# Folding the sign of the imaginary filter into its copy, and loading the third sequence of a Fourier filter and snake MLP kernel at other steps

## Chip, cores and metric

One core of one Trainium2 chip. The metric is the device time of one launch in microseconds, median of the runs shown. The kernel takes float32 inputs, works in float16 between the matmuls, and writes float32.

## The reference

```python
def _attn_ref(x, filt_r, filt_i):            # x: (8, 3008, 256), filters: (1505, 256)
    X = np.fft.rfft(x, axis=1)
    F = (filt_r + 1j * filt_i)[None, :, :]
    Y = X * F
    y = np.fft.irfft(Y, n=x.shape[1], axis=1)
    return y.astype(np.float32)

def _moe_ref(x, w_in, w_out, alpha):         # x: (24064, 256), w_in: (256, 2048)
    h = x @ w_in
    s = np.sin(alpha * h)
    g = h + s * s / (alpha + 1e-09)
    return (g @ w_out).astype(np.float32)
```

The second function takes the first one's result, 8 sequences of 3008 rows with 256 channels each, as one block of 24064 rows.

## The kernel before

**The spectral part** filters one sequence ("batch" b, 0 to 7) at a time. The length 3008 is split as 94 x 32, and the transform is done in four matmul stages with transfers between them.

- `load_x(b, ch)` (L138) loads a quarter of x on the POOL queue, and casts it to float16 on the way. From batch 2 on, the load waits for the last instruction of the MLP part that DVE was given before it (`marks["snake"]`, the STT below).
- `first(i)`, i = 0 to 15 (L178): one matmul `pa`, an eviction to `t1_h`, and after every fourth a store to the DRAM tile d1, on the SP queue (L186).
- `load_t2(g)`, g = 0 to 3 (L189): two POOL loads from d1, which turn rows into partitions.
- `forward(u)`, u = 0 to 11 (L196): two matmuls `pb`, an ACT cast to `xf`, and two SP transfers that write the halves of `xf` into `xs` with real and imaginary partitions crossed.
- `product(u)` and `cross(u)` (L211, L219): the complex product on DVE. `xf` times `f_t[0]`, plus `xs` times `f_t[1]`. `cross` waits for the transfers into `xs`.
- `inverse(w)` (L224): two matmuls `pc`, an eviction to `g`, and after every third two SP stores to the DRAM tile d2 (L239).
- `load_t4(ch)` (L242): a load from d2 on SP into the tile that the profile calls `t_a`.
- `last(u)`, u = 0 to 15 (L247): four matmuls `pd` and an eviction into columns of `y`, the input of the MLP part.

Batch 0 goes another way in a head of some 37 us: it turns tiles with DVE transposes, and multiplies by both filters in one instruction (L441), with the two products added by two accumulating matmuls, against the tables `e_t` and `e1_0`. `last_0` (L321) makes its columns of `y`, most of them spread one by one between the matmuls of the first steps; its half `cb` = 0 is evicted on ACT, `cb` = 1 on DVE.

The filter tile `f_t[k]`, k = 0 real and k = 1 imaginary, is loaded into half of the partitions only. `other_half(g, k, on_act)` (L383) copies it to the other half on DVE, in two groups g of 12 rows. Before the change the copy of the imaginary part is plain. The product of batch 0 wants it plain, with the sign in the table `e1_0`: `inverse_table` (L363) multiplies by a column `sign` of 0.125 and -0.125 (L360 to L362). The later batches want the lower half negated; `negate(i)` (L600) does that in place, after the products of batch 0, in two DVE instructions of 64x3072 (L603).

**Evictions.** `evac` (L157) puts PSUM into SBUF on ACT or DVE. Without an order from the caller, every third call goes to DVE and the others to ACT. Each call moves this count on, also one whose engine is ordered.

```python
        flip[0] = (flip[0] + 1) % 3
        if flip[0] if on_act is None else on_act:
```

**The MLP part** goes through y in 48 chunks of 512 columns (four of them of 384). `hidden(k, jb)` (L534) makes one of 16 blocks of a chunk: two accumulating matmuls `ph`, a cosine on ACT (L545), and one SCALAR_TENSOR_TENSOR on DVE (L546, "STT" below) into `v`. `project(k, u)` (L550) multiplies v by the second weights, 8 matmuls `po` each; after 16 or 32 of them ACT copies the result out (L566) and `store` sends it off (L586). For the first five chunks all these stores are issued on POOL, later ones on SP. The PSUM pools are `hps` with 4 slots for ph, `fps` with 2 slots for all spectral stages after the head, and `ops` with 2 slots for po.

**The order** is written out by hand. Time is counted in steps, 8 to a chunk. A step gives out two `hidden` blocks of chunk k and up to one `project` of chunk k - 1 (8 po). Everything else is a list of pairs "due step, piece" (`put`, L594). `slot(step)` (L634) runs between the two and `slot(step + 0.5)` at the end of the step; each gives out all pieces due, but stops at a second piece with matmuls unless that one is late by a step or more. Because the list is sorted by due step, a piece behind such a stop waits too. Every engine and every DMA queue works through its own pieces in the order in which they were given out. A step takes about 1.7 to 2.2 us.

In this order the pieces around the change fall as follows before it. The negates are given out at the end of step 13 and in the middle of step 14, around the evictions of `last_0`. The matmuls pa of batch 1 fall in steps 7 to 13, those of batch 2 in steps 36 to 47: the last one right after the ph of step 47. The loads of x of batch 2 fall in steps 22, 27, 32 and 37. The two crossed copies `xs` of batch 1 go out from step 17 (u = 0) to 31 (u = 11); its stores to d2 in steps 26, 30, 33 and 37, its loads of t4 in steps 38 (three) and 45. On SP the first d1 store of batch 2 stands just ahead of these three. The loads of t2 of batch 2 are given out in step 47, on POOL just ahead of the output store of chunk 4 (its second half: eight DMAs). The first pd of batch 1 is at the end of step 43, the first pb of batch 2 at the end of step 53.

Of the kernel before, what the change touches and what calls it, by code (L numbers as in the profile page):

```python
# [10 lines left out]
FP32 = mybir.dt.float32  # L11
# [3 lines left out]
ALU = mybir.AluOpType  # L15
# [47 lines left out]
def kernel(  # L63
# [10 lines left out]
    nc = tc.nc  # L74
# [17 lines left out]
    def pool(name, bufs, space=None):  # L92
        kw = {} if space is None else {"space": space}
        return ctx.enter_context(tc.tile_pool(name=name, bufs=bufs, **kw))

    cpool = pool("consts", 1)
# [18 lines left out]
    def by_half(t):  # L115

        return t.rearrange("p a (b c) -> p (a b) c", c=128)
# [16 lines left out]
    f_t = [filt_t[:, k] for k in range(2)]  # L134
# [22 lines left out]
    def evac(dst, src, on_act=None):  # L157
        flip[0] = (flip[0] + 1) % 3
        if flip[0] if on_act is None else on_act:
            marks["act"] = nc.scalar.copy(out=dst, in_=src)  # L160
        else:
            marks["dve"] = nc.vector.tensor_copy(out=dst, in_=src)  # L162
# [108 lines left out]
    e1_0 = by_half(t4_h[1])  # L271
# [24 lines left out]
    for g in range(2):  # L296
        gs = slice(12 * g, 12 * g + 12)
        for k, filt in enumerate((filt_r, filt_i)):
            for q in range(2):
                if (g, k, q) == (0, 1, 1):  # L300
# [3 lines left out]
                    out=f_t[k][64 * k + 32 * q:64 * k + 32 * q + 32, gs, :],  # L304
# [52 lines left out]
        nc.tensor.transpose(out=ps[:, 0:16], in_=rec, identity=id32)  # L357
        nc.vector.tensor_scalar(out=rec_t, in0=ps[:, 0:16], scalar1=-0.5, scalar2=None, op0=ALU.mult)

    sign = cpool.tile([128, 1], FP32)  # L360
    nc.vector.memset(sign[0:64], 0.125)
    nc.vector.memset(sign[64:128], -0.125)  # L362

    def inverse_table(g):

        gs = slice(8 * g, 8 * g + 8)
        ps = ops.tile([128, 8, 128], FP16, name=f"pse_{g}", tag="o")
        for i in range(8):
            for a in range(2):
                nc.tensor.transpose(out=ps[64 * a:64 * a + 64, i, :],  # L370
                                    in_=d_t[:, 8 * g + i, 64 - 64 * a:128 - 64 * a], identity=id16)
        nc.scalar.mul(e1_0[:, gs, :], ps, sign)

    warmed = []

# [7 lines left out]
    def other_half(g, k, on_act):  # L383

        gs = slice(12 * g, 12 * g + 12)
        evac(f_t[k][64 - 64 * k:128 - 64 * k, gs, :], f_t[k][64 * k:64 * k + 64, gs, :], on_act)

    warm_pe(10)
    def cast_x0(h):
# [6 lines left out]
    for i in range(16):  # L396
        own, tag = (fps, "f") if i % 3 == 2 else (hps, "h")
        ps = own.tile([128, 512], FP32, name=f"pa_0_{i}", tag=tag)
# [21 lines left out]
    for i in range(4):  # L420
        turn(t2_0[i // 2][:, :, 32 * (i % 2):32 * (i % 2) + 32], t1_0[:, :, 32 * i:32 * i + 32])
        if i > 1:
            other_half(0, i - 2, False)
# [56 lines left out]
    def weights_in(g):  # L480
# [4 lines left out]
        if g == 0:  # L485
            after(ins, marks["products"])

    [inverse_table(g) for g in range(2)]
    for i in range(6):
        forward_0(i)  # L490
        if i % 3 == 2:
            if i == 2: inverse_table(2)
            warm_pe((4, 0)[i // 3])
    for i in range(13):
        for e in {5: [(1,0,False)],6: [(1,1,False)]}.get(i, ()):
            other_half(*e)
        if i < 12:
            product_0(i)
        if i == 11:
            reciprocals()  # L500
        if i > 0:
            inverse_0(i - 1)
        if i + 6 < 12:
            forward_0(i + 6)
        if i == 12:
            turn_back(0)
# [87 lines left out]
    def put(at, fn, *args, pe=False):  # L594
        pending.append((at, len(pending), pe, fn, args))
# [1 line left out]
    for jb in range(12, 16):  # L597
        put(5 + 0.5 * (jb - 12), weights_out, jb, 1)

    def negate(i):  # L600

        gs = slice(12 * i, 12 * i + 12)
        nc.vector.tensor_scalar(out=f_t[1][0:64, gs, :], in0=f_t[1][0:64, gs, :],  # L603
                                scalar1=-1.0, scalar2=None, op0=ALU.mult)

    for i in range(2):
        put(13 + i, negate, i)
    for n0, n, at in ((6, 5, 1.5), (11, 4, 12.5), (15, 4, 14), (19, 4, 15.5), (23, 4, 17), (27, 5, 19)):
        put(at, last_0, n0, n, fps, "f", True)
    for b in range(1, B):  # L610
        s = s1 if b == 1 else Spectral(b)
        z = 48 * b
        if b > 1:
            for ch in range(4):
                put((22,27,32,37)[ch] if b == 2 else z - 92 + 7 * ch, s.load_x, ch)
        for i in range(16):
            put(6.9 + 0.35 * i if b == 1 else 36 + 0.66 * i if b == 2 else z - 67 + 0.66 * i, s.first, i, pe=True)
        for g in range(4):
            put(12.5 if b == 1 else max(z - 56, 46.5), s.load_t2, g)
        for u in range(12):  # L620
            inv = 23.5 + 1.25 * u if b == 1 else 59 + 2.1 * u if b == 2 else z - 40.8 + 2.3 * u
            fwd = inv - (6 if b == 1 else 6)
            put(fwd, s.forward, u, pe=True)
            put(fwd + (0.5 if b == 1 else 1.5), s.product, u)
            if s.fused:
                put(fwd + (4 if b == 1 else 4.5), s.cross, u)
            put(inv, s.inverse, u, pe=True)
        for ch in range(4):
            put(z - (9.5 if b == 1 and ch < 3 else (10.5, 10.5, 10.5, 3)[ch]), s.load_t4, ch)
        for u in range(16):  # L630
            put(z + (u - (5 if b == 1 else 6.5) if u < 4 else 2 * u - 9), s.last, u, pe=True)
# [59 lines left out]
```

## Time and profile before

| what | value |
|---|---|
| median of 3 runs | 785.87 us (785.68 to 786.81) |
| profiled execution | 785.97 us, its span 784.2 us |
| instructions | 16646 |
| granted TensorE clock, mean | 0.999 |
| ph matmuls (L541) | 1536, 387.8 us busy |
| po matmuls (L558) | 3008, 389.5 us busy |
| STT on DVE (L546) | 768, mean 671 ns |
| negate on DVE (L603) | 2, mean 946 ns |
| filter copies on DVE (L162, 64x3072) | 4, mean 956 ns |
| table multiplies on ACT (L372) | 3, mean 1126 ns |
| loads of x (L141) | 32, median 5.0 us from issue to landing |

The busy times of matmuls overlap, since they are pipelined; the time from one start to the next is what counts. In the timeline and in the chain of waits a row has a start and a length in microseconds, an engine (SPq and POOLq are the instructions that issue DMAs), a line of the kernel and a count. A `sign` or `filt_t` in a row is the tile's name in the program; `d` is d1 or d2, told apart by the line; `t` is t2 and `t_a` holds t4. In the windows, a row begins with the stretch and its length, then comes the busy time of PE, PEld, DVE, ACT and POOL with the number of instructions, the granted clock, the share of the DMA engines and GB/s.

### The profile page before, as it was taken

What the parts mean: (1) busy time and instruction counts of PE and PEld (TensorE: products, weight loads), DVE (VectorE), ACT (ScalarE), POOL (GpSimd) and SP (SyncE); (2) the same over time, 40 slices, a digit from 0 to 9 for tenths busy, and PEclk for the clock granted to TensorE, in tenths of its full rate; (3) what the DMA queues carried; (4) which work ended last, traced back from release to release, by engine and by line L of the source; (5) the groups of instructions that cost most, each with busy time, mean ns of one, the idle gap of its engine ahead of it and who ended that gap; (6) DMA issues with size and microseconds to landing.
All of it is one profiled execution on the core that took longest, in us unless ns stands there. A gap on an engine that the chain in (4) does not pass through costs nothing.

```text
span 784.2 us, 16646 instructions
## 1 busy us (share of the span) xinstructions
PE 771.1 (98%) x5799; PEld 535.2 (68%) x5799; DVE 655.7 (84%) x1169; ACT 617.6 (79%) x1211; POOL 113.3 (14%) x190
## 2 busy tenths in 40 slices
PE   7999999999999999999999999999999999999998
PEld 4757766676667766777666766767667776766666
DVE  7897996899878997799877998799977999777773
ACT  5797987888878887888877887788887887777674
POOL 6456443500020000200020000200002000000000
PEclk9999999999999999999999999999999999999999
DMA  9956577755564546654575454835556243421112
GB/s 214 281 112 164 124 142 213 158 124 121 163 174 89 129 105 190 148 122 108 131 202 114 103 115 131 226 87 118 119 161 176 65 98 80 117 61 29 41 41 54
DMA packets 86655, 100.99 MB, mean 129 GB/s; under 512 B 14896, under 2 KB 74294, under 8 KB 86572
## 3 DMA queue, kind: packets, MB, share of 16 engines
q1 hardware_dynamic: 74644, 71.11, 33.4%
q0 software_dynamic: 11712, 28.78, 19.4%
q8 instruction: 45, 0.74, 0.4%
q14 instruction: 38, 0.31, 0.1%
q10 hardware_dynamic: 216, 0.05, 0.0%
HBM read 55.72 MB, written 46.66 MB: 131 GB/s over the span
## 4 chain that ended last, share of the span: by engine, by line
PE 92%; DVE 3%; DMA 1%; ACT 1%; issue 1%; SPq 0%; ACTq 0%; DVEq 0%
PE po L558 40%; PE ph L541 39%; PE pa L181 3%; PE pd L254 2%; PE pb L201 2%; PE pc L232 2%; DVE v L546 2%; PE pc L453 1%; DMA al<-in_moe_alpha_dram 1%; ACT cos_all L545 1%; PE warm L381 1%; PE pb L431 1%; DMA t_a<-d 0%; SPq L586 0%; PE pa L399 0%
## 5 line engine op out<-in xcount | busy, mean ns | idle before, releaser
L546 DVE SCALAR_TENSOR_TENSOR v<-cos_all,ph 128x512 f16<-128x512 f32 (+1 forms) x768 | 482.9, 671 | 106.8 <-ACT cos_all L545 103.6
L545 ACT ACTIVATE cos_all<-ph 128x512 f32<-128x512 f32 (+1 forms) x768 | 411.2, 592 | 95.3 <-PE ph L541 94.3
L558 PE MATMUL po<-w,v 128*128 128x256 f16 x3008 | 389.5, 272 | 0.0
L541 PE MATMUL ph<-y,w 128*128 128x512 f16 (+1 forms) x1536 | 387.8, 374 | 1.6 <-DVE y L162 0.9
L558 PEld LDWEIGHTS <-v 128*128 128x128 f16 x3008 | 288.3, 98 | 78.3 <-issue 2.0
L541 PEld LDWEIGHTS <-w 128*128 128x128 f16 x1536 | 147.9, 98 | 103.9 <-issue 3.1
L566 ACT COPY o<-po 128x512 f32<-128x512 f32 (+1 forms) x97 | 55.6, 573 | 19.9 <-PE po L558 13.5
L586 POOL DMA_DIRECT2D out_dram<-o x67 | 35.0, 529 | 207.6 <-ACT o L566 205.4
L193 POOL DMA_DIRECT2D t<-d x56 | 36.3, 664 | 180.4 <-DMA out_dram<-o 98.7
L204 ACT CAST xf<-pb 128x512 f16<-128x512 f32 x84 | 50.0, 595 | 13.1 <-PE pb L201 12.3
L141 POOL DMA_DIRECT2D x<-in_x_dram x32 | 17.1, 537 | 259.7 <-PE pc L232 146.5
L160 ACT CAST t_h<-pa 96x512 f16<-96x512 f32 x74 | 43.3, 585 | 8.8 <-PE pa L181 8.5
L160 ACT CAST y<-pd 128x376 f16<-128x376 f32 (+1 forms) x82 | 39.5, 482 | 8.8 <-PE pd L254 5.3
L254 PEld LDWEIGHTS <-t_a 96*128 96x128 f16 x448 | 31.3, 97 | 19.8 <-DMA t_a<-d 1.4
L181 PE MATMUL pa<-x,wf_t 94*96 94x512 f16 x112 | 42.4, 381 | 0.6 <-ACT t_h L160 0.4
L160 ACT CAST g<-pc 128x512 f16<-128x512 f32 x61 | 36.2, 593 | 8.2 <-PE pc L232 7.8
L254 PE MATMUL pd<-wi_t,t_a 96*128 96x94 f16 x448 | 37.1, 204 | 1.1 <-DMA t_a<-d 1.1
L222 DVE TENSOR_TENSOR p<-p,xs 128x512 f16<-128x512 f16 x84 | 35.7, 425 | 2.9
L221 DVE TENSOR_TENSOR xs<-xs,filt_t 128x512 f16<-128x512 f16 x84 | 35.0, 417 | 0.0
L215 DVE TENSOR_TENSOR p<-xf,filt_t 128x512 f16<-128x512 f16 x84 | 35.0, 417 | 0.0
L201 PE MATMUL pb<-t,d_t 128*128 128x256 f16 x168 | 32.1, 272 | 0.2
L232 PE MATMUL pc<-p,e_t 128*128 128x256 f16 x168 | 32.1, 272 | 0.0
(66 smaller groups left out, 285.8 us busy)
## 6 DMA issues: line engine op xcount, KB each, us to landing
x<-in_x_dram POOLq DMA_DIRECT2D x30, 376.0 KB, 5.0
d<-t_h SPq DMA_DIRECT2D x28, 384.0 KB
t<-d POOLq DMA_DIRECT2D x56, 192.0 KB, 4.7
xs<-xf SPq DMA_DIRECT2D x168, 64.0 KB
d<-g SPq DMA_DIRECT2D x56, 192.0 KB
t_a<-d SPq DMA_DIRECT2D x28, 384.0 KB
out_dram<-o SPq DMA_DIRECT2D x92, 80.0 KB
w_out<-in_moe_w_out_dram SPq DMA_DIRECT2D x2, 1024.0 KB
```

Source lines behind the costliest of these rows:

```text
L160: marks["act"] = nc.scalar.copy(out=dst, in_=src)
L181: marks["pe"] = nc.tensor.matmul(out=ps[0:NK, :], lhsT=wf_t, rhs=self.x[ch][:, 2 * j:2 * j + 2, :], start=True, stop=True)
L193: nc.gpsimd.dma_start(out=self.t2[g][64 * p:64 * p + 64, :, :], in_=self.d1[a0:a0 + 6, :, :].rearrange("s n c -> n s c"))
L201: nc.tensor.matmul(out=ps[:, i, :], lhsT=d_t[:, s, :], rhs=self.t2[s // 6][:, s % 6, :], start=True, stop=True)
L204: nc.scalar.copy(out=self.xf[u], in_=ps)
L232: nc.tensor.matmul(out=ps[:, i, :], lhsT=e_t[:, 2 * w + i, :], rhs=pt[:, i, :], start=(k == 0), stop=(k == len(pr) - 1))
L254: nc.tensor.matmul(out=psv[:, i, :], rhs=wi_t, start=True, stop=True, lhsT=t4_h[ch // 2][0:NK, n0 % 16 + i, cb * 128:cb * 128 + 128])
L541: nc.tensor.matmul(out=ps[:, 0:n], lhsT=w1[:, cb, jb * 128:jb * 128 + 128], rhs=y_cols[:, cb, c0:c0 + n], start=(cb == 0), stop=(cb == 1))
L545: nc.scalar.activation(out=cs[:, 0:n], in_=ps[:, 0:n], func=AFT.Sin, bias=float(np.pi / 2))
L546: marks["snake"] = nc.vector.scalar_tensor_tensor(out=v[k][:, jb, 0:n], in0=cs[:, 0:n], scalar=-1.0, in1=ps[:, 0:n], op0=ALU.add, op1=ALU. ...
L558: nc.tensor.matmul(out=pso[k][:, t % 2, :], lhsT=v[k][:, jb, 128 * t:128 * t + 128], rhs=w2[:, jb, :], start=(jb == 0), stop=(jb == 15))
L566: nc.scalar.copy(out=o[:, i0:t % 2 + 1, :], in_=pso[k][:, i0:t % 2 + 1, :])
```

## The change

The imaginary filter's copy to the lower partitions is made with the factor -1 in the head, on DVE. The two `negate` instructions after batch 0 and their places in the order are gone. The table `e1_0` of batch 0 takes the factor -0.125 on all partitions, and the `sign` column with its two memsets is gone. `other_half` for k = 1 no longer calls `evac`, so two calls fewer move its count.

The loads of x of batch 2 get the due steps 22, 26, 30 and 34, its first stage 37 + 0.63 i in place of 36 + 0.66 i, and its loads of t2 step 47 in place of 46.5. For the later batches `z - 56` is the same number as before.

```diff
-    sign = cpool.tile([128, 1], FP32)
-    nc.vector.memset(sign[0:64], 0.125)
-    nc.vector.memset(sign[64:128], -0.125)
-
     def inverse_table(g):
...
-        nc.scalar.mul(e1_0[:, gs, :], ps, sign)
+        nc.scalar.mul(e1_0[:, gs, :], ps, -0.125)
...
     def other_half(g, k, on_act):
 
         gs = slice(12 * g, 12 * g + 12)
-        evac(f_t[k][64 - 64 * k:128 - 64 * k, gs, :], f_t[k][64 * k:64 * k + 64, gs, :], on_act)
+        if k == 0:
+            evac(f_t[0][64:128, gs, :], f_t[0][0:64, gs, :], on_act)
+        else:
+            nc.vector.tensor_scalar(out=f_t[1][0:64, gs, :], in0=f_t[1][64:128, gs, :],
+                                    scalar1=-1.0, scalar2=None, op0=ALU.mult)
...
-    def negate(i):
-
-        gs = slice(12 * i, 12 * i + 12)
-        nc.vector.tensor_scalar(out=f_t[1][0:64, gs, :], in0=f_t[1][0:64, gs, :],
-                                scalar1=-1.0, scalar2=None, op0=ALU.mult)
-
-    for i in range(2):
-        put(13 + i, negate, i)
...
-                put((22,27,32,37)[ch] if b == 2 else z - 92 + 7 * ch, s.load_x, ch)
+                put(22 + 4 * ch if b == 2 else z - 92 + 7 * ch, s.load_x, ch)
         for i in range(16):
-            put(6.9 + 0.35 * i if b == 1 else 36 + 0.66 * i if b == 2 else z - 67 + 0.66 * i, s.first, i, pe=True)
+            put(6.9 + 0.35 * i if b == 1 else 37 + 0.63 * i if b == 2 else z - 67 + 0.66 * i, s.first, i, pe=True)
         for g in range(4):
-            put(12.5 if b == 1 else max(z - 56, 46.5), s.load_t2, g)
+            put(12.5 if b == 1 else 47 if b == 2 else z - 56, s.load_t2, g)
```

## The prediction

> **What bounds the kernel now.** I read the page's shares first.
>
> ```profile
> PE 771.1 (98%) x5799; PEld 535.2 (68%) x5799; DVE 655.7 (84%) x1169; ACT 617.6 (79%) x1211; POOL 113.3 (14%) x190
> ...
> PE 92%; DVE 3%; DMA 1%; ACT 1%; issue 1%; SPq 0%; ACTq 0%; DVEq 0%
> ```
>
> TensorE is busy for 98% of the span and is 92% of the chain of waits, so an instruction taken off DVE is worth only what PE waits for it. I therefore cut the trace into steps (at the first ph matmul of each) and set each against its own work at full pace: 4 ph take 0.86 to 0.87 us at 512 columns and 0.65 at 384, 8 po 0.88, a pa 0.22, a pd 0.04. From step 9 to the end nearly every step is within 0.05 us of that. The large exceptions that the change can touch are steps 15, 16 and 43. Steps 14, 15, 16, 42 and 43, by windows (length, then each engine's busy time and instructions):
>
> ```profile
> 61.16:63.23 2.07, 2.07 (x21) 1.84 (x20) 1.92 (x3) 1.88 (x5) 0.00 (x0) 1.00 0.45 125
> 63.23:65.81 2.58, 2.24 (x24) 1.91 (x23) 2.40 (x4) 1.68 (x4) 0.28 (x1) 1.00 0.29 95
> 65.81:68.93 3.12, 2.22 (x23) 1.90 (x22) 1.94 (x4) 1.98 (x4) 3.12 (x6) 1.00 0.61 165
> 120.40:122.15 1.75, 1.75 (x15) 1.29 (x14) 1.49 (x4) 1.22 (x3) 0.00 (x0) 1.00 0.71 264
> 122.15:125.36 3.21, 2.08 (x20) 1.38 (x18) 1.34 (x3) 2.04 (x5) 0.40 (x1) 1.00 0.93 244
> ```
>
> Steps 14, 15 and 16 hold the same matmuls (4 ph, 8 pd, 8 po: 2.07 us); 15 and 16 lose 0.51 and 1.05. Step 43 holds 0.65 + 0.22 + 0.88 + 0.16 = 1.91 and takes 3.21: it loses 1.30. The clock column is 1.00, so none of it is clock. The chain of waits names both causes, first the two steps:
>
> ```profile
> 63.41 0.69 DVE v L546
> 64.09 0.86 DVE filt_t L603
> 64.96 0.46 DVE y L162
> 65.42 1.19 DVE v L546 x2
> 66.61 0.47 DVE y L162
> 67.08 0.04 issue
> 67.12 0.38 PE ph L541
> ```
>
> L603 is the second negate. It pushes back the y cast, two STTs and the next y cast, for which the ph at 67.12 waits: that ph reads these columns of y. In step 43 the chain runs over a load of t4, and the SP and POOL timelines show why it is late:
>
> ```profile
> 121.22 0.12 PE pa L181
> 121.33 3.80 DMA t_a<-d
> 125.13 0.05 issue
> 125.18 0.34 PE pd L254 x4
> ```
>
> ```profile
> 113.15 1.57 SPq L239 DMA_DIRECT2D d<-g  x2
> 115.62 0.32 SPq L186 DMA_DIRECT2D d<-t_h  x1
> 121.33 1.48 SPq L244 DMA_DIRECT2D t_a<-d  x3
> ```
>
> ```profile
> 113.60 0.52 POOL L141 DMA_DIRECT2D x<-in_x_dram  x1 [0.88 <-PE pa L181]
> ```
>
> The last store of d2 is issued in two halves at 113.15 and 114.15; the loads of t4 behind it wait for both. By the landing records the first half is in at 116.39, the second only at 121.19. Between them lies x chunk 3, issued at 113.60: its packets fill the engines from about 115.2 to 118.8, and the second half sends none from 115.9 to 118.8. In the same way the store issued at 105.11 sent nothing until 108.4, behind x chunk 2 (issued 104.89). A transfer that arrives behind an x chunk waits some 3 us here.
>
> **Negate gone: -0.47 us.** Two DVE instructions of 0.946 go from 61.45 and 64.01. The first costs nothing: the STT after it starts at 62.47, when its cosine is done at 62.44. Without the second, the y cast runs 64.01 to 64.55, the next STT at 64.55 (cosine done 64.51), but the one after it waits for its own cosine, which ACT finishes at 65.44 behind another y cast. It ends at 66.15, the needed y cast at 66.60, and ph starts near 66.65 instead of 67.12. So of 1.89 us of DVE work and 1.56 us of stall 0.47 comes back; then ACT is last. Bounds: 0.2, if the next limit bites (batch 1's first t2 pair lands at 70.36, and its pb starts at 70.83, so 0.47 ahead is the end of that cover; the d1 store before it goes out 0.2 later, see below), and 0.9, if the slot wait of 0.34 in step 15 goes as well. A PE wait of 0.33 just behind that pb, for an ACT cast, hides a late pb of that size, so I keep 0.47.
>
> **The sign in the head: 0.** The copies of filt_i cost 0.956 each (64x3072 COPY), a multiply of that shape is the negate's own row, 0.946: two times -0.01. The two memsets of 0.06 end at 3.26, ahead of 1.95 us in which DVE waits for x. The three ACT multiplies (1.126 each) read a constant in place of a column; no row shows that form, but the plain ACT copy of 512 (0.587) is within 0.03 of half of 1.126, and none of the three is in the chain: 0, bounds -0.1 and +0.1.
>
> **The rotation moves: 0.** Two calls of evac fewer in the head shift the three-beat rotation between ACT and DVE: each automatic eviction on DVE passes to the one before it in order. In steps 7 to 13 DVE then takes the casts i = 0, 3, 6, 9, 12, 15 of batch 1 instead of 1, 4, 7, 10, 13. For i = 15 the cast ends at 62.14 instead of 61.94, so the store of d1 and the loads of t2 behind it go 0.2 later (the bound above). For i = 0 it stands behind two STTs until 49.30; if the third pa took that PSUM slot it would start at 49.35 instead of 48.37, a stall of 0.98. But where an ACT slot came free first, PE in this trace waits for ACT (the pa at 52.72 does, though the older slot was DVE's), so I take 0. Later steps that lose 0.12 to 0.25 (at 195.1, 286.0, 290.4, 453.0, 564.1, 568.5) depend on the same rotation and go to other batches; six of them are 1.2 us, so half a microsecond either way is the bound.
>
> **x of batch 2 earlier: -1.30 us.** Each load is issued once its step's last STT is done plus 0.5. Chunk 3 goes from 113.60 to about 107.7, with packets from 109 to 112.3, clear of the d2 store at 113.15. That store then lands near 117 (the first d2 store's 768 packets took 2.1 us, 92.29 to 94.40). The loads of t4 also pass the d1 store of chunk 0, which moves behind them on SP; it was issued long before 121.33 and held them up by nothing, and now waits itself until about 118.5, with no reader before step 48. First t4 landing: 117.1 + 3.80 = 120.9. It is due at 123.85 (125.18 less 1.30), so 3 us to spare and the whole 1.30 returns. Lower bound 0: the store lands as late for another reason.
>
> The price is that chunks 1 and 2 now go at about 91.8 and 99.9, into the d2 stores issued at 90.96 and 99.19 and the crossed copies xs behind them, for which DVE waits in order with all STTs queued behind. xs 7 has its data at 95.05 and is read at 99.37, xs 10 at 103.90 and 107.20. One x chunk in front (3.2 us) leaves 1.1 and 0.1: hidden, just. Without that cover each further microsecond is a DVE stall.
>
> "DMA: Bandwidth & Descriptors" of the Trainium skill, section "Queues, rings and completion order", says that each engine takes turns between its queue rows packet by packet. By that rule the POOL load could not shut out SP's store; the empty stretch of 2.9 us in the trace differs, and the measurement decides. By the rule alone a separation of the two would save less.
>
> **First stage later: +0.2 us.** Sixteen pa move by a step on a PE that does them anyway. But the last pa of batch 2 goes from the start of step 47 to its end, and is cast by DVE: its d1 store goes out near 134.2 instead of 133.21 and lands near 137.2 (136.19 before). The loads of t2 move from step 47 to 48, and on POOL that is past the output store of chunk 4: eight issues of 0.52 to 0.55, 4.2 us, ready at 134.1 + 0.3. So t2 starts near 138.57 instead of 136.87. Its first pair landed at 141.16 and would at 142.86; pb of step 53 is due at 142.65. Stall 0.2; bounds 0 and 1.0 (if these stores take the 4.95 us from 142.02 to 146.97 that they took behind t2).
>
> **Sum.** -0.47 - 1.30 + 0.20 = -1.57. The profiled execution took 785.97 us (span 784.2 and 1.77 around it), 0.10 above the median of 785.87. From the median: 784.3.
>
> **Rivals.** *The t4 stall stays:* what speaks for it is that only one store in the trace shows the block from so near; against, the same hold behind chunk 2. Then -0.47 + 0.2: 785.6. *A lost slot or late t2:* the pa of step 8 waits for DVE, +0.98 (against: the pa at 52.72), or t2 lands a microsecond late: 785.2. *Slower, by crossing copies:* chunks 1 and 2 hit stores and xs together. The worst hold in the trace is the second half above, 4.4 us late against a landing near 116.8; with 1.4 us more of d2 packets in front xs 7 and xs 10 are 5.8 late and overrun their cover by 1.5 and 2.5. Less some 0.7 each that four ph slots cover, that is 2.6: 786.9. It decides from about 5 us of delay; against it, xs 8 behind chunk 1 today lands only 1.2 later than its neighbours.
>
> **Numbers.** Forecast 0.60 (own range 783.6 to 784.9), t4 stays 0.14, slot or t2 0.15, slower 0.11. The bound of 0.2% is 1.57 us, about what a measurement of this kernel can tell from no change, so the forecast sits on it. Faster: about three quarters of the forecast, 0.47, as the bounds of the negate and the rotation reach further below than above. Same: the rest and the two middle rivals, 0.43. Slower by over 0.2%, at least 787.44: 0.10. The range reaches down to the forecast with the rotation's half microsecond and 0.4 more from the negate (783.4), and up to 786.2.
>
> **What will show it.** Step 43 near 1.9 us with no wait on t_a, and the last d2 store's second half landing near 117. Step 16 near 2.6 with y's cast ending 0.5 earlier, behind a cosine. POOL's eight stores ahead of t2 near 134, and a pb wait of a few tenths in step 53. DVE without waits at the reads of xs 7 and xs 10. Wrong, if PE waits for xs, if step 8 grows by a microsecond, or if the loads of t4 are still issued near 121.

## The result, and the profile after

The changed kernel takes 784.76 us in the median of 12 runs (783.84 to 786.17). In the same comparison the kernel before takes 786.43 us (785.68 to 788.10, 12 runs): a ratio of 0.9977, 95% interval 0.9968 to 0.9986. A second comparison, made with the last experiments, gave 785.37 against 786.75 us, 0.9982 (0.9974 to 0.9991). So about 0.2% of the time is gone, just at the size that this kernel's measurement can tell. The profiled execution took 784.61 us, its span 782.8 us where it was 784.2.

The shares first, on the page of the changed kernel:

```profile
PE 771.7 (99%) x5799; PEld 535.3 (68%) x5799; DVE 654.4 (84%) x1165; ACT 617.0 (79%) x1211; POOL 113.3 (14%) x190
...
PE 93%; DVE 2%; POOL 1%; ACT 1%; DMA 1%; issue 1%; SPq 0%; ACTq 0%; POOLq 0%; DVEq 0%
```

PE's busy time is what it was; a percent of the chain passed from DVE to PE, and POOL has one now, which it had not before. The same five steps as before the change (14, 15, 16, 42, 43), by windows: the stretch and its length, then the busy time of PE, PEld, DVE, ACT and POOL, the granted clock, the DMA share and GB/s.

```profile
61.45:63.52 2.07, 2.07 (x21) 1.83 (x20) 1.71 (x3) 1.46 (x4) 0.00 (x0) 1.00 0.28 87
63.52:65.72 2.20, 2.20 (x24) 1.91 (x22) 1.82 (x3) 1.67 (x4) 0.00 (x0) 1.00 0.49 145
65.72:68.78 3.06, 2.23 (x24) 1.91 (x23) 1.84 (x3) 2.00 (x5) 2.87 (x5) 1.00 0.43 129
120.20:121.95 1.75, 1.75 (x15) 1.28 (x13) 1.47 (x4) 0.87 (x2) 0.00 (x0) 1.00 0.71 202
121.95:123.86 1.91, 1.91 (x18) 1.46 (x17) 1.03 (x3) 1.71 (x4) 0.00 (x0) 1.00 1.02 380
```

Steps 15 and 16 together went from 5.70 to 5.26, and step 43 from 3.21 to 1.91, its full pace. The chain of waits of the changed kernel in steps 15 and 16 (start, length, engine, line):

```profile
64.20 0.61 ACT cos_all L545
64.81 0.43 ACT y L160
65.23 0.51 ACT cos_all L545
65.74 0.02 issue
65.77 0.69 DVE v L546
66.46 0.47 DVE y L162
66.92 0.04 issue
66.97 0.38 PE ph L541
```

Where the second negate stood, two cosines with a y cast between them are now in the chain: ACT came to be last, as forecast, so of the DVE time taken out only these tenths return. For step 43, the SP timeline of the changed kernel, and the POOL timeline with its x chunks (start, length of the row, line, count, idle time before):

```profile
112.78 1.57 SPq L239 DMA_DIRECT2D d<-g  x2
116.64 1.87 SPq L244 DMA_DIRECT2D t_a<-d  x3
118.62 2.85 SPq L186 DMA_DIRECT2D d<-t_h  x2
```

```profile
107.69 0.52 POOL L141 DMA_DIRECT2D x<-in_x_dram  x1 [2.55 <-DVE v L546]
...
132.87 4.16 POOL L586 DMA_DIRECT2D out_dram<-o  x8 [4.96 <-ACT o L566]
137.10 5.20 POOL L193 DMA_DIRECT2D t<-d  x8
```

x chunk 3 goes at 107.69, clear of the store of d2 at 112.78, whose second half lands at 116.48 by the landing records (121.19 before); t4 is issued at 116.64 and lands at 120.33, 3.4 us ahead of its pd at 123.69. The last two rows are the output stores that t2 now stands behind.

A thing that was not forecast is at step 9. The chain there, and two rows of the waits around it:

```profile
48.06 1.85 POOL w L514
49.92 0.02 issue
49.94 1.28 DVE v L546 x2
51.23 0.61 DVE t_h L162
51.84 0.04 issue
51.88 0.38 PE pa L181
```

```profile
DVE v L546 <- POOL w L514: 1.0, 1, 1.0
...
PE pa L181 <- DVE t_h L162: 0.4, 1, 0.4
```

An STT waits 1.0 us for POOL's last multiply of the second weights (L514), because its `v` takes the buffer that held them; the cast of a pa stands behind it on DVE, and a pa waits for that cast. Worked out for each step as its length less its matmuls at full pace, what PE lost in the two profiled executions:

| steps | before, us | after, us | difference | forecast |
|---|---|---|---|---|
| up to the first ph (its time) | 36.86 | 36.52 | -0.34 | 0 |
| 9 | 0.04 | 0.60 | +0.56 | 0 (rotation) |
| 15 and 16 | 1.66 | 1.21 | -0.45 | -0.47 |
| 41 and 60 | 0.31 | 0.25 | -0.06 | 0 (rotation) |
| 43 | 1.35 | 0.05 | -1.30 | -1.30 |
| 53 | 0.05 | 0.05 | 0 | +0.20 |
| 80, 126, 128, 212, 270, 272 | 1.20 | 0.24 | -0.96 | 0 (rotation) |
| 68, 84, 116, 174, 176, 260 | 0.23 | 1.24 | +1.01 | 0 (rotation) |
| all steps | 21.91 | 20.82 | -1.09 | -1.57 |

"All steps" begins with the first ph; what it holds beyond the rows above is +0.11, spread over small ones. The full pace is taken a little tighter than the common spacing, so that a step without a stall still shows 0.03 to 0.05; by the median spacing of each kind of matmul the two sums are 9.3 and 8.2, and the differences in the table are the same to 0.05. Only differences are used below. The rows of step 60 and later are the rotation of evictions: small stalls that change places. The first row differs from launch to launch: over the 14 profiled executions of this study the first ph starts between 36.26 and 39.40 us, in no order of the kernels. So two rows answer to the forecast to a few hundredths, and two were wrong in opposite directions.

### The profile page after: what moved, and what is told of

Read it like the earlier page. It is cut to its first block, busy times and chain, and to the rows that moved or that the text cites. A ratio compares the mean times of both kernels' runs of the same rounds, so it can differ in the third digit from the quotient of the medians.

```text
span 782.8 us, 16640 instructions
## 1 busy us (share of the span) xinstructions
PE 771.7 (99%) x5799; PEld 535.3 (68%) x5799; DVE 654.4 (84%) x1165; ACT 617.0 (79%) x1211; POOL 113.3 (14%) x190
## 4 chain that ended last, share of the span: by engine, by line
PE 93%; DVE 2%; POOL 1%; ACT 1%; DMA 1%; issue 1%; SPq 0%; ACTq 0%; POOLq 0%; DVEq 0%
PE po L558 41%; PE ph L541 40%; PE pa L181 3%; PE pd L254 2%; PE pb L201 2%; PE pc L232 2%; POOL w L514 1%; PE pc L453 1%; DMA al<-in_moe_alpha_dram 1%; DVE v L546 1%; PE warm L377 1%; PE pb L431 1%; SPq L586 0%; POOL w L482 0%; PE pa L399 0%
```

## Experiments

Each was run beside the kernel before on the same chip, and compared with it. "Stalls" below are PE's losses by step as in the table, from the profiled execution; they tell a few tenths of a microsecond apart, which medians with intervals of 0.1% do not. In most comparisons the medians lie further apart than the stalls (1.56 against 0.43 us for the times of batch 2 alone, 2.52 against 1.74 for the best order below). The one trace of the kernel before is of an execution of 785.97 us, and its medians beside the experiments are 786.4 to 786.8; what those executions lose more, no trace here shows.

**The sign alone.** The changed kernel with the times of batch 2 as before, and with one line that puts the rotation back:

```diff
             nc.vector.tensor_scalar(out=f_t[1][0:64, gs, :], in0=f_t[1][64:128, gs, :],
                                     scalar1=-1.0, scalar2=None, op0=ALU.mult)
+            flip[0] = (flip[0] + 1) % 3
...
-                put(22 + 4 * ch if b == 2 else z - 92 + 7 * ch, s.load_x, ch)
+                put((22,27,32,37)[ch] if b == 2 else z - 92 + 7 * ch, s.load_x, ch)
```

> The sign alone, with the eviction rotation and batch 2's steps as before. Theory (the second negate held up the y cast and ACT is next): steps 15 and 16 together lose 1.15 to 1.25 us against 1.56 to 1.66 before, ph of step 16 still waits for the y cast, behind a cosine of ACT; step 43 keeps its stall of 1.3; time 0.3 to 0.6 us lower, a ratio of 0.9993 to 0.9996, too small to tell by time alone. Rival (all DVE time comes back): both stalls vanish, 1.6 us, ratio 0.998. Step 9: if its stall of 0.56 in the changed kernel comes from the rotation, it is absent here; if it comes from w_out's load landing late on this launch, it is here whenever POOL's last weight multiply ends later than about 49.3 us.

786.33 against 786.76 us, ratio 0.9992 (0.9980 to 1.0004). Steps 15 and 16 lose 1.22, 0.44 less than before; step 43 keeps a stall (1.57), and step 9 has none, which tells little, as POOL's last multiply ended only 11.23 after the first ph in this launch (13.39 in the changed kernel's). The negate is worth what its chain says, and the 1.89 us of DVE work are not.

**The times of batch 2 alone.** The kernel before with the changed due steps of x, first stage and t2, and with its negates.

> Batch 2's steps alone, negates kept. Theory (x chunk 3 no longer stands before the last d2 store): step 43 at 1.9 us, t4's first load issued 4 us earlier against its step, no wait for xs 7 and xs 10, pb of step 53 without a wait or with less than 0.3; steps 15 and 16 lose 1.6 as before; time 1.0 to 1.4 us lower, ratio 0.9982 to 0.9987. Rival (crossing copies or late t2 take it back): a DVE wait before the reads of xs of 1 us or more, or a pb wait of 0.5 or more in step 53, ratio above 0.9995.

785.20 against 786.76 us, 0.9975 (0.9965 to 0.9986). Step 43 is at 0.05, and steps 15 and 16 as before. But step 53 loses 0.94, which it does not in the changed kernel: its first pair of t2 lands at 141.49, where the one of the changed kernel lands at 141.04.

**x chunk 3 alone, and the first stage alone.** In the one the kernel before has its x loads at (22, 27, 32, 34), in the other its first stage and t2 go a step later and x stays at (22, 27, 32, 37).

> Only x chunk 3 of batch 2 moves, from step 37 to 34; chunk 2 stays at 32. Theory: this alone frees the last d2 store, which lands within 3.5 us of its first issue instead of 8; step 43 at 1.9 us, time 1.1 to 1.4 us lower, ratio 0.9982 to 0.9987. Rival (the order of the t4 loads and the d1 store on SP, moved by the later first stage, is what counts): step 43 keeps 1 us or more of stall, ratio above 0.9993.

785.91 us, 0.9980 (0.9965 to 0.9994). Step 43 loses 0.05, step 53 too: chunk 3 by itself frees the stall.

> Only the first stage and the t2 loads of batch 2 move; the x chunks stay at 22, 27, 32, 37. Theory: the last d2 store still waits behind x chunk 3, step 43 keeps a stall of 1.0 to 1.4 us; t2 starts behind the store on POOL as in the changed kernel, pb of step 53 waits 0 to 0.3; ratio 0.9997 to 1.0005. Rival (SP order counts): step 43's stall gone, ratio near 0.9985.

785.51 us, 0.9978 (0.9967 to 0.9989). Here the theory fell: step 43 has no stall either. The POOL and SP timelines of this run show why:

```profile
112.86 0.52 POOL L141 DMA_DIRECT2D x<-in_x_dram  x1 [0.31 <-PE ph L541]
```

```profile
112.76 1.58 SPq L239 DMA_DIRECT2D d<-g  x2
119.20 1.28 SPq L244 DMA_DIRECT2D t_a<-d  x3
```

Chunk 3 is issued at 112.86, 0.74 earlier than before the change, since fewer pieces stand ahead of it in the list. It now goes 0.10 behind the first half of the d2 store, where before the change it is 0.45 (113.60 and 113.15). The store's packets go out beside those of x, sparsely at first, and both halves wait (landed at 118.49 and 119.05); but the second is in 6.3 us after the first issue and not 8.0, and t4 is in at 122.98, half a microsecond ahead of its pd at 123.50. The stall of 1.30 hung on some 0.35 us in the place of a load against a store. Step 53 loses 0.74 here.

**Is it the d1 store that holds t4?** The kernel before, with its first three loads of t4 ahead of the d1 store of batch 2's chunk 0 on SP:

```diff
-            put(z - (9.5 if b == 1 and ch < 3 else (10.5, 10.5, 10.5, 3)[ch]), s.load_t4, ch)
+            put(z - (10.1 if b == 1 and ch < 3 else (10.5, 10.5, 10.5, 3)[ch]), s.load_t4, ch)
```

> The kernel before with one pair of SP's queue swapped: the three t4 loads of batch 1 ahead of batch 2's first d1 store. x chunk 3 stays at step 37. Theory (two transfers delay the last d2 store: x chunk 3 keeps its second half out, and then that half shares the engines with the d1 store's packets): the second half lands 1.5 to 2.5 us earlier than 8.0 us after the first issue, t4's first load lands 2 us earlier, and step 43 keeps 0 to 0.3 us of its 1.35: ratio 0.998 to 0.9988. Rival (the forecast's reading, x chunk 3 alone, the d1 store holds up nothing): 1.2 to 1.4 us stay, ratio 0.9995 to 1.0005.

785.81 against 786.62 us, 0.9986 (0.9975 to 0.9996). The SP timeline and the chain of this run:

```profile
113.20 1.57 SPq L239 DMA_DIRECT2D d<-g  x2
121.33 1.25 SPq L244 DMA_DIRECT2D t_a<-d  x3
122.69 0.35 SPq L186 DMA_DIRECT2D d<-t_h  x1
```

```profile
121.27 0.06 PE pa L181
121.33 3.61 DMA t_a<-d
124.94 0.05 issue
124.98 0.34 PE pd L254 x4
```

The loads stand first and are still issued at 121.33, for the second half of the d2 store lands at 121.17 as before (x chunk 3 is issued at 113.66). Step 43 loses 1.10 in place of 1.35: a load of 3.61 in place of 3.80 is all that comes back. What holds the store is the x chunk.

**The rotation alone.** The kernel before, with a line that moves the count as the change does:

```diff
+        flip[0] = (flip[0] - k) % 3
```

> The kernel before with the eviction count set as in the changed one, and nothing else. Theory (the cast i = 3 of batch 1 on DVE stands behind STTs that wait for POOL's last w_out multiply): steps 8 and 9 lose 0.67 in all if that multiply ends less than 12.3 us after the first ph, and 0.5 to 0.6 more if it ends 13.4 us after it; of the late small stalls six of 0.1 to 0.25 move to other steps, their sum within 0.3; step 43 keeps 1.35 and steps 15 and 16 lose 1.6 or 0.2 more; ratio 0.9997 to 1.0007. Rival (the rotation costs a PSUM slot at step 8 in every launch): step 8 or 9 1.0 us longer wherever that multiply ends.

786.05 against 786.62 us, 0.9992 (0.9979 to 1.0004). Steps 8 and 9 lose what they lose before; the slot rival of the forecast, 0.98 in step 8, is not there. The late small stalls are in just the places of the changed kernel. And a group is new: steps 40, 41, 42, 44, 47 and 48 lose 1.33 together, where they lose 0.31 before. Step 16 loses 0.14 more than before. Step 43 is at 0.05, for two reasons: PE comes to it later by the new stalls, and chunk 3 goes out 0.16 behind the d2 store's first half (113.91 and 113.75), so that the second half is in 6.45 us after the first issue. t4 lands at 124.40, by 1.1 us sooner than before when both are counted from the first ph, and is there for the pd at 125.00:

```profile
113.91 0.52 POOL L141 DMA_DIRECT2D x<-in_x_dram  x1 [0.58 <-PE ph L542]
```

```profile
113.75 1.58 SPq L239 DMA_DIRECT2D d<-g  x2
120.35 1.77 SPq L244 DMA_DIRECT2D t_a<-d  x3
```

The chain at step 40:

```profile
116.43 1.29 DVE v L547 x2
117.72 0.61 DVE t_h L162
118.32 0.04 issue
118.36 0.38 PE pa L181
```

It is the picture of step 9: the rotation puts a cast of the first stage on DVE behind two STTs, and a pa waits for it. The changed kernel has only 0.22 of this (step 41).

**POOL's order in the head.** The changed kernel, with the first load of batch 1's x one multiply later, so that POOL gets on while that load waits for the second weights to land:

```diff
-    for step in ([(weights_in, g) for g in range(3)] + [(s1.load_x, 0), (weights_in, 3), (s1.load_x, 1),
-                 (weights_in, 4), (s1.load_x, 2), (weights_in, 5), (s1.load_x, 3)]
+    for step in ([(weights_in, g) for g in range(4)] + [(s1.load_x, 0), (weights_in, 4), (s1.load_x, 1),
+                 (weights_in, 5), (s1.load_x, 2), (s1.load_x, 3)]
```

> The changed kernel with two of POOL's pieces reordered in the head: the fourth and the later weight multiplies go ahead of the x load that waits for w_out's landing. Theory (POOL sat idle for that landing, and its last multiply ends too late for the STTs of step 8): the last w_out multiply ends 1 to 2 us earlier against the first ph, at 10.5 to 12 us after it; step 9 at its 2.13 us without stall in this launch; the x loads of batch 1 are not waited for; ratio to before 0.9970 to 0.9978. Rival (step 9's stall is the rotation's alone): step 9 keeps 0.5 us or more.

784.44 against 786.62 us, 0.9972 (0.9962 to 0.9981). The stall of step 9 is gone (0.04), though in this launch the load of x came free later than in the changed kernel's (38.09, that is 1.52 after the first ph, against 0.66). Step 36 has a new 0.18: DVE waits 0.51 us there for the crossed copy xs 10, and the pc behind it waits for DVE.

**More of steps 15 and 16.** The changed kernel, with the `last_0` pieces of steps 12.5 and 14 due at 11.5 and 13, and batch 1's inverse stage slightly later.

> The changed kernel with two groups of batch 0's last stage a step earlier, and batch 1's forward and inverse stage a half step later. Theory (the ph of step 16 waits for the y cast of a group that is made in step 15, with ACT last in the chain): with that group made in step 14, steps 15 and 16 lose under 0.3 us together in place of 1.2; the pb of batch 1 waits for nothing; ratio to before 0.9962 to 0.9972. Rival (two PSUM slots are too few for pa and pd in one step, or t2 lands too late for pb): step 13 or the step of the first pb gains 0.7 us or more, ratio above 0.9975.

786.29 us, 0.9994 (0.9985 to 1.0004): the gain of the change is gone. Steps 15 and 16 lose 0.08 together, as hoped; but step 13 loses 1.96, step 20 0.65 (0.27 in the changed kernel) and step 32 0.24. The waits of PE around step 13:

```profile
PE pa L181 <- DVE t_h L162: 0.8, 1, 0.8
PE pd L343 <- ACT t_h L160: 0.5, 1, 0.5
```

The pa of batch 1 and the pd of batch 0 share the two slots of `fps`, and one step earlier they meet there.

**The last four** belong together. First the changed kernel again:

> The changed kernel once more, whole, to see which of its stalls are the order's and which the launch's. Theory: step 43 free (near 0.05), step 16 near 1.04 and step 15 near 0.17 in every launch, but the 0.56 of step 9 varies with the landing of w_out (0.56 if POOL's last multiply of w_out ends 13.2 us or more after the first ph, nothing if it ends before 12.5), and step 53 varies between nothing and 0.9 with the landing of the last d1 store and t2. Ratio 0.997 to 0.998. Rival: the 0.56 of step 9 belongs to the order and comes back at the same size whenever POOL's multiply ends.

The ratio is given above. Step 43 loses 0.05, steps 15 and 16 1.21, step 9 0.45, step 53 0.17 (0.05 in the first profile; the first pair of t2 landed 4.18 us after the first issue, where it was 3.94). The 0.45 fits the size of POOL's lateness, not a fixed price: counted from the first ph, POOL's last multiply ended at 13.24 here, at 13.39 in the changed kernel's first profile (0.60) and at 13.23 in the run with the earlier `last_0` pieces (0.45). Less 0.04, each is what the end lies beyond 12.83. With 12.38, 11.82 and 11.20 (three other kernels with the moved rotation) step 9 loses 0.04. Without the moved rotation an end at 13.76 (the first stage alone) costs nothing, and one at 14.15 (chunk 3 alone) costs 0.30: the bound there is about 1.0 us later.

Then POOL's order as above with the sign, and the two things left over crossed: the rotation put back or moved, and the first stage with t2 of batch 2 as before (x at 22, 27, 32, 34) or a step later (x at 22, 26, 30, 34).

> The parts that paid alone: sign in the copy with the rotation put back, x of batch 2 at 22, 27, 32 and 34 with its first stage and t2 as before, and the w_out multiplies on POOL ahead of the last x loads of batch 1. Theory: -0.44 (steps 15, 16), -1.30 (step 43), steps 9, 41 and 53 without a new stall, so 1.7 to 1.8 us below the kernel before on the same chip, ratio near 0.9977, a few tenths below the changed kernel. Rival: the last stores and loads of POOL decide anew, and one of steps 9, 36 or 53 takes 0.5 us or more; then no better than the changed kernel.

> As e10_parts with one line less: the rotation of evictions moves as in the changed kernel. Theory: with POOL's multiplies early the rotation's price in step 9 is gone, and only small stalls change places (41 appears, 60 goes, the late ones move to 68, 84, 116, 174, 176 and 260): within 0.3 us of e10_parts, either sign. Rival: the rotation costs half a microsecond whatever POOL does.

> All of the changed kernel but its rotation, which is put back, and with POOL's w_out multiplies early: against e10_parts it is the first stage and t2 of batch 2 a step later (and x at 22, 26, 30, 34) alone. Theory: the price of the later t2 belongs to the order and shows wherever PE comes to step 53 without having lost time before it: a stall of 0.5 to 0.9 in step 53, as in e2_times and e4_first (0.94, 0.74), so 0.5 to 0.9 above e10_parts, 784.7 to 785.2. Rival: that stall is the launch's (the landing of the last d1 store), step 53 is free here (0.05) and the time that of e10_parts, 784.2.

| rotation | first stage, t2 | median, us | against before | ratio (interval) | lost in all steps | steps 40 to 48 | step 53 |
|---|---|---|---|---|---|---|---|
| put back | as before | 784.23 (5 runs) | 786.75 | 0.9965 (0.9953 to 0.9977) | 20.17 | 0.62 | 0.05 |
| moved | as before | 785.36 | 786.75 | 0.9983 (0.9973 to 0.9993) | 20.98 | 1.49 | 0.05 |
| put back | a step later | 784.73 | 786.84 | 0.9971 (0.9956 to 0.9985) | 20.99 | 0.60 | 0.87 |
| moved | a step later | 784.44 | 786.62 | 0.9972 (0.9962 to 0.9981) | 20.43 | 0.81 | 0.05 |

The last row is the run with POOL's order alone, from above. The stalls of the first row are 1.74 below those before the change, as expected (1.7 to 1.8). The expectation for the second row (within 0.3 us) was wrong: its stalls are 0.81 above the first's. That for the third was right against its rival. By the stalls each of the two edits costs 0.8 us by itself, and both together cost 0.26: each takes away most of what the other costs. By time the rows cannot all be told apart, as their intervals overlap. With the rotation moved, the casts of the first stage stand badly in steps 40 to 48; a step later they stand well. With the first stage a step later, t2 is late; with the rotation moved it is not, and the timelines of the third row's run show what differs:

```profile
133.49 0.30 SPq L186 DMA_DIRECT2D d<-t_h  x1
```

```profile
133.27 4.14 POOL L587 DMA_DIRECT2D out_dram<-o  x8 [4.92 <-ACT o L567]
138.44 5.19 POOL L193 DMA_DIRECT2D t<-d  x8 [1.02 <-PE pd L254]
```

The last d1 store goes out 0.22 behind the first output store, its packets run from 134.49 to 137.27, 2.78 us, and t2 waits 1.02 behind the eight. (The row names a pd, but t2 starts 0.68 after the landing of the d1 store, 137.76, as it does before the change and in the other two runs of this kind.) In the changed kernel (SP issues it at 132.97, 0.10 behind the first of the stores, because the last cast is on DVE and not on ACT behind the copy of `o`) they take from 133.78 to 135.96, 2.18 us, and t2 follows the stores at once. The other two runs of this kind say the same: 2.81 and 2.51 us of packets, and stalls of 0.94 and 0.74. In all three the pb starts 0.13 to 0.14 after the landing of its first pair of t2. In two of them the view names ACT's copy of `o` for this wait, but in the third that copy is still running when the pb starts, so it is the landing that counts. That this tenth of a microsecond in the order of issue is the cause, and not another transfer, was not tried apart.

## Why the prediction was right, and where it was not

The forecast of 784.3 us was 1.57 below its median; the result is 1.67 below the median it was measured against. Of its steps:

- **Negate gone, -0.47: right.** -0.45 in the changed kernel, -0.44 alone, and with ACT next in the chain as the forecast had it. The bounds of 0.2 and 0.9 were not needed.
- **The sign in the head, 0: right as far as it can be seen.** The two multiplying copies take 0.954 each, and the three multiplies by a constant on ACT 1.041 in place of 1.126. The first ph moves by more from launch to launch than any of it; so -0.34 in the table is no gain of the change.
- **The rotation moves, 0: this step failed.** Its reading of step 8 was right (no lost slot in any run), and so was "half a microsecond either way" for the late steps, which came to +0.05. But it looked for the price in PSUM slots alone. An eviction put on DVE also inherits what stands ahead of it there: in step 9 an STT that waits for POOL, 0.56 and 0.41 in two launches, and in steps 40 to 48 pairs of STTs, 0.8, if the first stage had not moved as well. In the trace of before the first could be seen coming: POOL's last multiply ended at 48.79, 11.93 after the first ph, and the STT behind it stood right ahead of the cast that the forecast itself placed there; what it lacked was by how much that end moves between launches, against a cover of 0.9 (12.83 less 11.93).
- **x of batch 2 earlier, -1.30: right to the hundredth**, and for the reason given: chunk 3 alone does it, the d1 store ahead of t4 does not (0.25 of 1.35). The store's second half landed at 116.48 where "near 117" was forecast, t4 at 120.33 where 120.9 was. The rival that the crossed copies would stall DVE came to next to nothing: DVE waits once, 0.24 us, at xs 10, where the forecast had left a cover of 0.1, and PE loses nothing by it; with POOL's order the same wait is 0.51 and costs step 36 some 0.15. That chunk 3 had to go much earlier was not so; 0.35 us against the store were enough, with half a microsecond to spare in place of 3.4. (The forecast's 123.85 for the pd is 123.88 by its own terms.)
- **First stage later, +0.20: mis-sized, and the wrong way in the whole.** Its times were right (POOL's stores from 132.87, t2 at 137.10 against a forecast 137.07 if shifted by the 1.5 us gained), but pb came due 0.2 later against them, as one pa more falls between (from the start of step 47 to that of step 53 PE takes 9.64 us, 9.43 before, and 9.63 in the run of the times alone), and the pair landed sooner (3.94 after the first issue against 4.29), so nothing was left of it in one launch and 0.12 in the other. The cover is thin: t2 was free to go, 0.68 after the landing of the d1 store, within a tenth of the end of the eight output stores. By itself, without the moved rotation, the same step costs 0.74 to 0.94, inside its upper bound of 1.0.

By the stalls the sum of -1.57 was too large by 0.48: the rotation took back 0.55 and some 0.1 went in small ones, and the first stage's 0.20 was not paid. The rest of what the two profiled executions differ by is a head that was 0.34 shorter in that launch. The medians are 1.67 and 1.38 us apart in the two comparisons, and their intervals reach from 0.7 to 2.5; that they came within 0.2 of the forecast is luck. The single terms for the negate and for x are what the experiments confirm. The best version here is the first row of the last table, with the sign, chunk 3, POOL's order and nothing else: by its stalls (20.17 of 21.91 before), and against the changed kernel on the same chip, where each of its 5 runs (784.01 to 784.46, median 784.23) is below each of the 11 of the other (784.60 to 786.73, median 785.37). Against the last two rows of the table time does not tell.

## What to carry to other kernels

When a piece leaves an order in which engines are dealt out by turns, every later piece changes hands; look for the ones that come to stand in a queue behind an instruction that waits, not only for the buffers they hold, or put the count back (by the stalls worth 0.8 us here with the first stage as before, but a loss of 0.6 with it a step later). A stall behind a transfer can hang on the place of another queue's transfer within a third of a microsecond: find which load stands in front and move that one alone. And a gain of a tenth of a percent is better read from the stalls by step of one trace than from medians, as long as what the launch itself moves (the head, landings) is set apart, and as long as it is said what the medians show beyond it.

## What the runs showed of the hardware

- A load of x with its cast (94 rows of 4096 bytes as written, on POOL) held up a store that SP issued within half a microsecond of it, and how much hung on the order. Issued 5 us ahead, the load had no part in it: the second half of the d2 store landed 3.7 us after the first issue (112.78 to 116.48). Issued 0.10 or 0.16 behind the first half, its packets and the store's went out side by side, and it took 6.3 and 6.45 us. Issued 0.45 or 0.46 behind (the kernel before, the sign alone, t4 first), the second half sent no packet for 2.4 to 3.4 us and landed after 8.0 (113.15 to 121.19).
- The Trainium skill ("DMA: Bandwidth & Descriptors", section "Queues, rings and completion order") says that an engine takes turns between queue rows packet by packet, and that a whole packet is typically some 9 to 17 descriptors. The 94 rows of x are about six for each of 16 engines; were these six one packet, the rule would allow an empty stretch, which the forecast took to be against it. No run here shows how the rows are packed or which engine sent what, and why 0.3 us in the order makes this difference stays open.
- The end of POOL's multiplies, which hangs on when the weights land, lay between 11.23 and 14.15 us behind the first ph over ten launches with POOL's first order, and between 11.18 and 12.38 over four with the other. Cover in the head that is thinner than that spread is no cover.
- A store of 96 packets of 4096 bytes took 1.8 to 1.9 us of packets with no output store near it (before the change, and in the six other runs of that order), 2.2 to 2.3 when issued 0.10 or 0.11 behind the first of eight stores on POOL (four runs), and 2.5 to 2.8 when issued 0.22 behind it (three).
- An ACT multiply of 128x1024 by a constant took 1.041 us, by a column 1.126. The Trainium skill ("ScalarE: Activation LUTs", section "What ACT_TABLE_LOAD costs") gives some 93 ns for each operand that is a column; the 85 measured here are near it. Forecast at nothing, it was worth nothing either, as none of the three is in the chain.
